# Identity products in TensorE's waits, keys asked for by GpSimd, and one scaling moved, in a fused delta-rule and maxout kernel

## Chip, core and metric

The kernel runs on one core of one Trainium2 chip. The metric is the device time of one execution in microseconds (us), as a median over runs. Engines are called as in the profile: PE (TensorE's matrix multiplications, with PEld for its weight loads), DVE (VectorE), ACT (ScalarE), POOL (GpSimd) and SP (SyncE, which here only issues DMAs).

## What is computed

A delta-rule attention is followed by a feed-forward layer with a maximum over three products. All is float32.

```python
# q, k, v: (4, 8, 768, 48); beta: (4, 8, 768)
k_n = k / (np.linalg.norm(k, axis=-1, keepdims=True) + 1e-06)
state = 0                                  # (4, 8, 48, 48)
for t in range(768):
    y[:, :, t] = q[:, :, t] @ state        # by batch and head
    v_old = state applied to k_n[:, :, t]
    state += beta[t] * outer(k_n[:, :, t], v[:, :, t] - v_old)
x = y.transpose(0, 2, 1, 3).reshape(3072, 384)
h = np.maximum(np.maximum(x @ w1, x @ w2), x @ w3)   # 384 -> 768
out = h @ w_out                                      # 768 -> 384
```

## The kernel before

The sequence of 768 steps is cut into 12 chunks of 64. Within a chunk the recurrence becomes small matrix products and a triangular inverse. A chunk has two units (n = 2c and 2c+1), each of two batches by eight heads; four units (two chunks) make a group, and there are six groups, m = 0 to 5. A group's 512 tokens then go through the feed-forward layer, `ffn(m)`.

The order on every engine is written out by hand, in the order in which the Python code emits instructions. There are three stretches.

The opening, before the first `ffn`, loads keys, turns them (`turn`, p_t), forms products of keys with keys and queries (`gram` and `keys`, p_g), and inverts the first group's triangles in `solve(0)`, a chain of small DVE steps (L570 and L574). ACT and DVE copy the inverse into `ut` (L589, L591); POOL does so for the second chunk. Half blocks are then joined: `halves_z` (p_e), `halves_u` (p_f, with the negations L686 on DVE and L688 on ACT), `join_z` (p_z), `join_u` (p_j). `new` makes the new values u (p_u), `to_y` the outputs (p_y), `to_x` turns these into `xt` (p_x, copied by L880 on ACT and L881 on DVE).

`ffn(0)` is a generator with 31 periods, i = 0 to 30. In each it emits one hidden product, p_h (L930), with its copy or maximum (L938 on ACT, L944 on DVE), or one output product, p_o (L962). Between two of them the loop places links of the recurrence, from two tables: `FIRST` (group 0 and the keys and queries of the first units) and `EARLY_LINKS` (group 1). A letter with a number is one link: `z1` is `join_z(1)`, `k1` is `old_k(1)` (p_k), `T2` turns the queries of unit 2, `P2` forms their products, `S1` makes one step of `solve`. The loop also converts the weights from 64-bit floats piece by piece (`weights`: ACT L232 and L241, POOL L236, DVE L251 and L255, POOL L259; a piece's last three steps come with the following piece), loads keys, and scales a chunk's values by the norms of its keys (`prep_values`, POOL L292 on `v_t`). It makes solve(2), and the subtractions `less_first` (L887).

The later `ffn(m)`, m = 1 to 5, take their links from `LINKS`. There, POOL loads the keys (L118) and values (L137), and both SP and POOL load turned blocks (L401). `p1` in `LINKS` calls `prep_values` for the group ahead; for a chunk that has been scaled before, it does nothing.

`kpad` holds the keys of eight units: unit n lies in place n mod 8 for n below 12. So unit 8 takes the place of unit 0, which `step(0)` (p_s, L795) reads last. PSUM has two buffers for p_h, p_o and the filler products (`ps_ffn`), and three of two banks for the others (`ps_two`).

`busy(n, of)` multiplies the identity with `of` n times into one PSUM tile that nobody reads. The kernel before calls it once, at the very start, with 6.

Of the kernel before, what the change touches and what calls it, by code (L numbers as in the profile page):

```python
# [21 lines left out]
def kernel(  # L22
# [105 lines left out]
    def load_k(n, queues=one_queue):  # L128
        load(k, kpad[place(n)], n, queues)
# [167 lines left out]
    def prep_values(c):  # L297

        if c in nrms:
            scale(c, nrms.pop(c))  # L300
# [37 lines left out]
    def first_norms():  # L338
        norm(nrm_0, ksum_0, small("root0", 2, 2, H), small("newton0", 2, 2, H))
# [7 lines left out]
    def by_par(t):  # L347
        return t.rearrange("p (j two) x -> p two j x", two=2)
# [77 lines left out]
    def masked(t, of, engine=nc.vector):  # L426
        engine.tensor_tensor(  # L427
            out=by_par(t), in0=of,
            in1=mask[:, None, None, :].to_broadcast([128, 2, NP, C]), op=ALU.mult,
        )  # L430

    def gram(n, parts=(0, 1), queues=one_queue, copy=nc.scalar.copy, later=False):
        kqt, g = kqts[n], n % 2
        p_g = ps_two("p_g")

        whole = len(parts) == 2 and not g
        for j in range(NP):
            for par in range(2):
                for bb in range(2):
                    kq = kqt[dims(par), j, bb ^ g]  # L440
                    for i in (0,) if whole else parts:
                        c0 = j * 128 + i * C
                        nc.tensor.matmul(  # L443
                            p_g[
                                rows(bb ^ (g * i)), par, c0 : c0 + C * (1 + whole)
                            ],
                            kq[:, 0],
                            kq if whole else kq[:, i],
                        )
        p_v = p_g.rearrange("p two (j i t) -> p two j i t", j=NP, i=2)  # L450
        if 1 in parts:
            pt = pts[n] = square("pt")
            if later:
                copy(by_par(pt), p_v[:, :, :, 1])
            else:
                masked(pt, p_v[:, :, :, 1])
        if 0 not in parts:
            return
        at = ats[n] = square("at")
        copy(by_par(at), p_v[:, :, :, 0])  # L460
        if queues:
            to_dram(n, queues)
# [171 lines left out]
    def turn_t1(c):  # L634

        t, u_t = t1[c % NU], ut[c % NU]
        nc.vector.transpose(out=t[:, 0], in_=u_t[:, 0, :, 0:BL])
        for bb in range(2):
            nc.vector.transpose(
                out=t[block(1 - bb), 1], in_=u_t[block(bb), 1, :, 0:BL]  # L640
            )
# [28 lines left out]
    def halves_z(c):  # L670
        if c > 1:
            halves_t(c)
        at = [ats[2 * c + g] for g in range(2)]
        second = ut[c % NU].rearrange("p g h (f two x) -> p g h f two x", two=2, x=HB)
        for hs, p_v, copy in heads_of(c, "p_e", BL):
            for i, h in enumerate(hs):
                for bb, g in TILES:
                    r = rows(bb)
                    nc.tensor.matmul(
                        p_v[rows(bb ^ g), g, i], at[g][r, h], second[r, g, h, :, 1]  # L680
                    )
            copy(zs[c % NU][:, :, span(hs)], p_v)
# [7 lines left out]
    def halves_u(c):  # L690
        t, z = fine.pop(c), zs[c % NU]
        for hs, p_v, _ in heads_of(c, "p_f", BL):
            for i, h in enumerate(hs):
                for bb, g in TILES:
                    r = rows(bb ^ g)
                    nc.tensor.matmul(p_v[rows(bb), g, i], t[g][r, h], z[r, g, h])
            for f in (0, 1):
                for bb in range(2):
                    r = block(bb, f, HB)
                    negated(  # L700
                        bb,
                        ut[c % NU][r, :, span(hs), BL * f + HB : BL * (f + 1)],
                        p_v[r, :, :, HB * f : HB * (f + 1)],
                    )

    def join_z(c):
        at = [ats.pop(2 * c + g) for g in range(2)]
        z, second = zs[c % NU], ut[c % NU][:, :, :, BL:C]
        for hs, p_v, _ in heads_of(c, "p_z", BL):
            for i, h in enumerate(hs):  # L710
                for bb, g in TILES:
                    r = block(bb, 1)
                    nc.tensor.matmul(  # L713
                        p_v[block(bb ^ g), g, i], at[g][r, h, 0:BL], second[r, g, h]
                    )
            nc.scalar.copy(z[block(0), :, span(hs)], p_v[block(0)])
            copy = nc.vector.tensor_copy if c < 2 else nc.scalar.copy
            copy(z[block(1), :, span(hs)], p_v[block(1)])

    def join_u(c):  # L720
        z, t = zs[c % NU], t1[c % NU]
        u12 = ut[c % NU][:, :, :, BL:C]
        for hs, p_v, _ in heads_of(c, "p_j", BL):
            for i, h in enumerate(hs):
                for bb, g in TILES:
                    r = block(bb ^ g)
                    nc.tensor.matmul(p_v[block(bb), g, i], t[r, g, h], z[r, g, h])  # L727
            for bb in range(2):
                negated(bb, u12[block(bb), :, span(hs)], p_v[block(bb)], c)
# [36 lines left out]
    def new(c):  # L766
        rhs = rhss.pop(c)
        u = us[c] = both("u", D, 2)
        for hs, p_v, copy in heads_of(c, "p_u", D):
            for i, h in enumerate(hs):  # L770
                for bb, g in TILES:
                    nc.tensor.matmul(  # L772
                        p_v[rows(bb ^ g), g, i],
                        ut[c % NU][rows(bb), g, h],
                        rhs[rows(bb), g, h],
                    )
            copy(u[:, :, span(hs)], p_v)
        if c + NU < 2 * FINE:
            for bb in range(2):
                corner = ut[c % NU][block(bb), :, :, BL:C]  # L780
                zero = kpad[0][block(bb), None, 0:1, D : D + 1]
                nc.scalar.copy(corner, zero.to_broadcast(corner.shape))
# [193 lines left out]
    def some(gen, n):  # L976
        for _ in range(n):
            if next(gen, gen) is gen:
                break
# [59 lines left out]
    keys(7)  # L1039
    turn(1, (1,))  # L1040
    gram(1, (1,), None, later=True)
    for _ in range(2):
        fetch(nc.sync)
    blocks(1)
# [3 lines left out]
    some(solving, HB + 1)  # L1048
    halves_t(0)
    halves_z(0)  # L1050
    first_norms()
    for c in range(2):
        scale(c, nrm_0[:, c])
    some(conv, 1)
    halves_u(0)
    turn_t1(0)
    join_z(0)
    masked(pts[0], by_par(pts[0]))
    join_u(0)
    masked(pts[1], by_par(pts[1]))  # L1060
    old_k(0)
    old_q(0)
    some(solving, 1)
    new(0)
    some(conv, 1)
    fetch(nc.sync)
    to_y(0)
# [1 line left out]
    fetch(nc.sync)  # L1069
    halves_z(1)  # L1070
    to_x(0)
    some(conv, 1)
    fetch(nc.sync)
    halves_t(1)
# [18 lines left out]


    FIRST = {
        0: "f1 s0 T2 S1 S1", 1: "z1 d1 S1 k1 P2 T3 S1 S1", 2: "j1 S1 S1 S1",
        3: "P3 S1 q1 S1 S1", 4: "u1 T4", 5: "y1", 6: "s1 T5 P4", 7: "x1 T6",
        8: "P5 T7", 10: "P6", 12: "P7",
    }
# [5 lines left out]
    )  # L1105
    MADE = dict(V=load_v, P=prep_values)
    UNIT = dict(t=turn, g=gram, K=load_k, L=lambda n: load_blocks(n, nc.sync))
    OF_KEYS = dict(S=lambda n: some(solving, n), T=lambda n: turn(n, (1,)), P=lambda n: gram(n, (1,)))

    def links(m, names):  # L1110
        for name in names.split():
# [23 lines left out]
    for i, _ in enumerate(ffn(0)):  # L1135
        if i - 1 in CONVERTED:
            fetch(nc.sync)
        queries(FIRST.get(i, ""))
        links(1, EARLY_LINKS.get(i, ""))
        if i in CONVERTED:  # L1140
            some(conv, 1)
        if i in (4, 5, 6):
            some(solving, (4, 2, 1)[i - 4])
        if i in (5, 7):
            prep_values(i // 2)
        if 7 <= i < 11:
            load_k(i + 1)
        if i == 0:
            load_v(3)
        if i == 12:  # L1150
            load_q(11)
        if i in (10, 18):
            load_v(4 + i // 18)
        if i == 18:
            blocks(2)
        if i == 21:
            solving = solve(2)
            some(solving, 1)
        if i in (22, 25):
            prep_values(4 + i // 25)  # L1160
        if 21 < i < 27:
            some(solving, 3)
        if i >= 27:
            some(solving, 4 if i < 30 else 5)
        if i in (27, 28, 29):
            load_blocks(i - 15, nc.sync)
        if i in (18, 19, 20, 22, 25, 27):
            less_first((18, 19, 20, 22, 25, 27).index(i))
        if 27 <= i < 30:
            turn_first((2 * (i - 27), 2 * (i - 27) + 1))  # L1170
# [48 lines left out]
```

## Time and profile before

| | us |
|---|---|
| median of 6 runs | 544.28 (542.42 to 547.78) |
| the profiled execution's own time | 544.39 |
| its span | 542.7 |
| PE busy | 505.6 (93%) |
| DVE busy | 317.2 (58%) |
| POOL busy | 178.9 (33%) |
| ACT busy | 154.6 (28%) |
| mean granted PE clock | 0.955 of full speed |

The span is what the records of the profile cover; the profiled execution took 1.7 us more. A row of the order of time reads: start, duration, engine, line and operation, what is written from what, shape and count, and in brackets the idle time before it with what ended it. A row of a table of stretches reads: the stretch, its length, then busy time and number of instructions on PE, PEld, DVE, ACT and POOL, then the granted PE clock, the DMA engines' busy share and GB/s.

### The profile page before, as it was taken

What the parts mean: (1) busy time and instruction counts of PE and PEld (TensorE: products, weight loads), DVE (VectorE), ACT (ScalarE), POOL (GpSimd) and SP (SyncE); (2) the same over time, 40 slices, a digit from 0 to 9 for tenths busy, and PEclk for the clock granted to TensorE, in tenths of its full rate; (3) what the DMA queues carried; (4) which work ended last, traced back from release to release, by engine and by line L of the source; (5) the groups of instructions that cost most, each with busy time, mean ns of one, the idle gap of its engine ahead of it and who ended that gap; (6) DMA issues with size and microseconds to landing.
All of it is one profiled execution on the core that took longest, in us unless ns stands there. A gap on an engine that the chain in (4) does not pass through costs nothing.

```text
span 542.7 us, 18538 instructions
## 1 busy us (share of the span) xinstructions
PE 505.6 (93%) x8096; PEld 312.7 (58%) x8096; DVE 317.2 (58%) x701; ACT 154.6 (28%) x285; POOL 178.9 (33%) x303
## 2 busy tenths in 40 slices
PE   6657788999979999999999999999999999999996
PEld 5546677876536555556654566565565555654453
DVE  5877898776899552199762489661989313101100
ACT  5536364575302233210133220153101331010100
POOL 7216146234293280665093766231330000000000
PEclk9756898999989999999997999999999999999999
DMA  8882847885024591544393546474323402130011
GB/s 110 186 164 77 150 116 166 177 197 132 17 55 103 129 179 28 120 121 116 86 180 67 126 116 148 107 128 87 89 71 77 80 2 57 49 73 1 0 22 36
DMA packets 118848, 53.49 MB, mean 99 GB/s; under 512 B 100976, under 2 KB 113456, under 8 KB 118768
## 3 DMA queue, kind: packets, MB, share of 16 engines
q1 hardware_dynamic: 109872, 40.01, 34.7%
q0 software_dynamic: 6784, 11.92, 9.9%
q8 instruction: 63, 1.03, 0.8%
q10 hardware_dynamic: 2112, 0.39, 0.5%
q14 instruction: 17, 0.14, 0.1%
HBM read 39.17 MB, written 13.11 MB: 96 GB/s over the span
## 4 chain that ended last, share of the span: by engine, by line
PE 78%; DVE 13%; ACT 3%; issue 3%; DMA 2%; SPq 1%; POOL 0%; ACTq 0%; DVEq 0%; POOLq 0%
PE p_h L930 35%; PE p_o L962 25%; PE p_g L443 3%; PE p_m L910 2%; DVE tmp L570 2%; PE p_y L814 2%; PE p_u L772 2%; PE p_k L744 2%; PE p_q L744 2%; SPq L118 1%; PE p_j L727 1%; PE p_s L795 1%; DVE y_bl L574 1%; DMA kmore<-in_k_dram 1%; PE p_z L713 1%
## 5 line engine op out<-in xcount | busy, mean ns | idle before, releaser
L930 PE MATMUL p_h<-xt,w_sb 128*128 128x512 f32 (+1 forms) x522 | 222.3, 571 | 7.9 <-DVE h L944 3.6
L930 PEld LDWEIGHTS p_h<-xt,w_sb 128*128 128x128 f32 x522 | 97.3, 195 | 95.9 <-issue 86.8
L962 PE MATMUL p_o<-wo_sb,h 128*128 128x384 f32 x288 | 97.8, 489 | 0.0
L944 DVE TENSOR_TENSOR h<-h,p_h 128x512 f32<-128x512 f32 (+1 forms) x48 | 29.6, 618 | 95.8 <-PE p_h L930 95.7
L962 PEld LDWEIGHTS p_o<-wo_sb,h 128*128 128x128 f32 x288 | 53.7, 190 | 35.7 <-issue 0.5
L570 DVE TENSOR_TENSOR tmp<-x_bl,y_bl 128x31 f32<-128x31 f32 (+20 forms) x139 | 51.5, 371 | 4.1
L968 ACT COPY o_sb<-p_o 128x384 f32<-128x384 f32 x24 | 11.5, 478 | 140.6 <-PE p_o L962 134.5
L574 DVE TENSOR_TENSOR y_bl<-y_bl,tmp 128x31 f32<-128x31 f32 (+20 forms) x139 | 47.5, 342 | 4.8
L940 ACT ACTIVATE h<-p_h 128x512 f32<-128x512 f32 x30 | 17.9, 597 | 91.0 <-PE p_h L930 86.7
L962 PE MATMUL p_o<-w_sb,xt 128*128 128x384 f32 x120 | 42.0, 486 | 0.0
L401 POOL DMA_DIRECT2D turned<-in_q_dram x72 | 39.1, 550 | 4.7 <-POOL turned L396 2.6
L443 PE MATMUL p_g<-kqt 48*64 48x64 f32 (+1 forms) x1216 | 29.7, 241 | 10.9 <-DVE nt_bl L268 3.7
L443 PEld LDWEIGHTS p_g<-kqt 48*64 48x64 f32 x1216 | 25.1, 141 | 18.6 <-ACT kqt L372 7.8
L962 PEld LDWEIGHTS p_o<-w_sb,xt 128*128 128x128 f32 x120 | 22.8, 190 | 15.9
L427 DVE TENSOR_TENSOR pt<-p_g,mask 128x512 f32<-128x512 f32 x22 | 15.2, 691 | 20.3 <-PE p_g L443 20.1
L292 POOL TENSOR_TENSOR v_t<-v_t,nrm 128x768 f32<-128x768 f32 x12 | 17.8, 1489 | 27.9 <-DVE nrm L271 13.5
L236 POOL TENSOR_SCALAR mant<-mant 128x384 f32<-128x384 f32 x24 | 13.1, 547 | 41.5 <-ACT mant L232 41.5
L802 DVE TENSOR_TENSOR st<-st,p_s 48x768 f32<-48x768 f32 (+1 forms) x18 | 17.1, 950 | 15.4 <-PE p_s L795 15.2
L137 POOL DMA_DIRECT2D v_t<-in_v_dram x12 | 9.9, 830 | 41.8 <-PE p_u L772 41.8
L259 POOL TENSOR_TENSOR w_sb<-mant,up 128x384 int32<-128x384 int32 x18 | 17.9, 997 | 12.8 <-DVE mant L255 12.8
L396 POOL MEMSET turned<- 128x96 f32 x18 | 3.3, 193 | 53.9 <-DVE kqt L417 53.9
L118 POOL DMA_DIRECT2D kpad<-in_k_dram x24 | 16.3, 687 | 11.5 <-PE p_s L795 11.5
(151 smaller groups left out, 621.6 us busy)
## 6 DMA issues: line engine op xcount, KB each, us to landing
w_bits<-in_moe_w_dram SPq DMA_DIRECT2D x18, 384.0 KB, 5.8
out_dram<-o_sb SPq DMA_DIRECT2D x48, 96.0 KB, 2.2
turned<-in_q_dram POOLq DMA_DIRECT2D x72, 48.0 KB, 2.6
y_x<-y SPq DMA_DIRECT2D x16, 192.0 KB
qall<-y_x SPq DMA_DIRECT2D x32, 96.0 KB, 3.0
at_d<-at SPq DMA_DIRECT2D x80, 32.0 KB, 2.2
ut<-y_d SPq DMA_DIRECT2D x40, 64.0 KB, 2.6
qall<-in_q_dram SPq DMA_DIRECT2D x24, 96.0 KB, 3.9
```

What stands on the lines that cost most here:

```text
L118: queues[bb].dma_start(out=dst[rows(bb ^ g), :, 0:D], in_=src[2 * bb + g, :, c * C : (c + 1) * C, :].rearrange("h p d -> p h d"),)
L259: nc.gpsimd.tensor_tensor(out=dst.bitcast(I32), in0=mant_v.bitcast(I32), in1=up_v, op=ALU.add)
L292: nc.gpsimd.tensor_tensor(out=vts[c], in0=vts[c], in1=nrm[:, :, :, None].to_broadcast([128, 2, H, D]), op=ALU.mult,)
L401: (queue, nc.gpsimd)[i].dma_start(out=t[p0 : p0 + 32, bb, at : at + NP * 2 * D].rearrange("p (j x) -> p j x", j=NP), in_=(k, q)[i][2 * bb ...
L443: nc.tensor.matmul(p_g[rows(bb ^ (g * i)), par, c0 : c0 + C * (1 + whole)], kq[:, 0], kq if whole else kq[:, i],)
L570: nc.vector.tensor_tensor(out=t_v, in0=row.to_broadcast(t_v.shape), in1=column.to_broadcast(t_v.shape), op=ALU.mult,)
L574: nc.vector.tensor_tensor(out=rest, in0=rest, in1=t_v, op=ALU.subtract)
L744: nc.tensor.matmul(p_b[rows(bb), par, c0 : c0 + D], kqt[g][dims(par), j, bb ^ g, i], st[dims(par), bb ^ g, g, j],)
L930: nc.tensor.matmul(p_h, w_sb[i][:, t, f * 128 : (f + 1) * 128], xt[:, t, lo : lo + w], start=(t == 0), stop=(t == KT - 1),)
L940: nc.scalar.activation(out=h, in_=p_h, func=mybir.ActivationFunctionType.Relu)
L944: nc.vector.tensor_tensor(out=h, in0=h, in1=p_h, op=ALU.max)
L962: nc.tensor.matmul(p_o, stays, moves, start=(n == 0), stop=(n == len(terms) - 1))
```

## The change

Three things are done in one edit. First, `busy` is called at more places: seven in the opening, with 49 products in all, and, by a new letter `B` in `FIRST`, 4 and 6 in period 1 of `ffn(0)`. Second, the keys of units 8 to 11 are asked for by POOL, those of units 8 and 9 in period 1 and those of 10 and 11 in period 7; before, SP asked for them one unit a period in periods 7 to 10. Third, the values of chunk 5 are no longer scaled in period 25 of `ffn(0)`; `p1` of `LINKS` does it in period 5 of `ffn(1)`.

```diff
@@ opening
     gram(1, (1,), None, later=True)
+    busy(22, ident)
     for _ in range(2):
         fetch(nc.sync)
...
     halves_z(0)
+    busy(4, ident)
     first_norms()
...
     halves_u(0)
+    busy(4, ident)
     turn_t1(0)
     join_z(0)
+    busy(2, ident)
     masked(pts[0], by_par(pts[0]))
     join_u(0)
+    busy(7, ident)
     masked(pts[1], by_par(pts[1]))
...
     new(0)
+    busy(4, ident)
     some(conv, 1)
     fetch(nc.sync)
     to_y(0)
...
     to_x(0)
+    busy(6, ident)
     some(conv, 1)
@@ links of ffn(0)
-        0: "f1 s0 T2 S1 S1", 1: "z1 d1 S1 k1 P2 T3 S1 S1", 2: "j1 S1 S1 S1",
+        0: "f1 s0 T2 S1 S1", 1: "B4 z1 d1 S1 k1 P2 B6 T3 S1 S1", 2: "j1 S1 S1 S1",
...
-    OF_KEYS = dict(S=lambda n: some(solving, n), ...
+    OF_KEYS = dict(B=lambda n: busy(n, ident), S=lambda n: some(solving, n), ...
@@ loop of ffn(0)
-        if 7 <= i < 11:
-            load_k(i + 1)
+        if i in (1, 7):
+            for n in range(2):
+                load_k(8 + 2 * (i > 1) + n, (nc.gpsimd, nc.gpsimd))
...
-        if i in (22, 25):
-            prep_values(4 + i // 25)
+        if i == 22:
+            prep_values(4)
```

More of the change, by code (lines that the diff above doesn't have):

```diff
@@ L1107 @@
     UNIT = dict(t=turn, g=gram, K=load_k, L=lambda n: load_blocks(n, nc.sync))
-    OF_KEYS = dict(S=lambda n: some(solving, n), T=lambda n: turn(n, (1,)), P=lambda n: gram(n, (1,)))
+    OF_KEYS = dict(B=lambda n: busy(n, ident), S=lambda n: some(solving, n), T=lambda n: turn(n, (1,)), P=lambda n: gram(n, (1,)))
     def links(m, names):
```

## The prediction

> **What bounds the kernel now.** I read the page first, then stretches of 2 us over the opening, the waits of TensorE, and the order of time on TensorE, VectorE and GpSimd around each wait.
>
> ```profile
> span 542.7 us, 18538 instructions
> ...
> PE   6657788999979999999999999999999999999996
> ...
> PEclk9756898999989999999997999999999999999999
> ...
> q8 instruction: 63, 1.03, 0.8%
> ```
>
> TensorE (PE) is busy 93% of the span and nearly always from about 88 us on. Only the opening, one dip near 150 us and one near 285 us have room. PE's waits, from the answer on waits (us in all, times, longest):
>
> ```profile
> PE p_e L679 <- ACT ut L589: 4.7, 2, 4.1
> PE p_h L930 <- DVE h L944: 3.6, 2, 2.9
> PE p_h L930 <- issue: 2.0, 1, 2.0
> PE p_j L727 <- issue: 1.8, 1, 1.8
> ```
>
> The stretches show the opening's second trouble: after the hole at 26 us the granted clock (third figure from the right) is a half.
>
> ```profile
> 24.00:26.00 2.00, 1.33 (x52) 1.02 (x44) 1.77 (x7) 1.14 (x2) 0.00 (x0) 1.00 0.29 49
> 26.00:28.00 2.00, 0.23 (x15) 0.05 (x4) 1.81 (x6) 0.58 (x1) 0.00 (x0) 0.51 0.43 60
> 28.00:30.00 2.00, 0.00 (x0) 0.00 (x0) 1.93 (x3) 0.79 (x1) 0.00 (x0) 0.50 0.46 67
> ...
> 48.00:50.00 2.00, 2.00 (x42) 1.89 (x35) 1.46 (x2) 1.29 (x3) 1.32 (x3) 0.52 0.69 195
> 50.00:52.00 2.00, 0.75 (x5) 0.52 (x4) 1.21 (x3) 1.81 (x5) 1.34 (x2) 1.00 0.49 115
> ```
>
> It stays a half until 49.9 us; p_f, p_z, p_u, p_y, p_e and p_x run there at about twice their later times (p_u 2.35 us against 1.15, p_y 1.96 against 1.15). From 52 to 83 us the chain of waits is VectorE (DVE) nearly throughout (1.8 to 2.0 busy in every 2 us), after that PE. At 150 us, in order of time:
>
> ```profile
> 149.59 2.91 POOL L292 TENSOR_TENSOR v_t<-v_t,nrm 128x768 f32<-128x768 f32 x2
> 149.74 1.40 DVE L574 TENSOR_TENSOR y_bl<-y_bl,tmp 128x60 f32<-128x60 f32 x1
> 151.17 1.43 DVE L570 TENSOR_TENSOR tmp<-x_bl,y_bl 128x87 f32<-128x87 f32 x1
> 153.74 0.68 DVE L944 TENSOR_TENSOR h<-h,p_h 128x512 f32<-128x512 f32 x1
> 154.56 7.08 PE L930 MATMUL p_h<-xt,w_sb 128*128 128x512 f32 x12 [2.95 <-DVE h L944]
> ```
>
> Two tiny DVE steps last as long as the two scalings on GpSimd (POOL) beside them; elsewhere the same steps take 0.22 to 0.25 us. L944 comes late for it, and PE stands 2.95 us, then runs at half clock from 155.7 to 159.1.
>
> [...] the trace's changes (15.78, 22.61, 26.02, 49.91, 63.57, 66.98, 84.05, 87.46, ...) lie whole multiples of 3.41 us apart. Windows busy 1.97 to 2.14 us out of 3.41 went either way; the ones that restored the clock were busy throughout. [...] the added products are ordinary matmuls, and no run so far shows 22 of them. [...] PE's "issue" waits at 39.6, 61.7, 107.4, 201.3 and 283.5 us come after 1217, 2241, 4289, 7361 and 9921 recorded instructions, all 193 above a multiple of 256. From the entry into one block to the next being there took 2.6 to 4.9 us where it was waited for (7.1 once, in the opening); a PE that runs 256 small instructions faster than that stands.
>
> **The change part by part.** All is added to the profiled execution, 544.39 us with a span of 542.7; the median of the six runs is 544.28, so 0.1 lower.
>
> *Fillers in the opening (49 identity products: 22, 4, 4, 2, 7, 4, 6).* A product is two passes. At half clock the opening's 12 passes started over 2.72 us: 0.453 us a product. At full clock four transposes of 128 columns start over 0.46 us (121.61 to 122.07): 0.115 a pass, 0.23 a product. The 22 start at 26.2 us, after the last p_g, and p_e can start in earnest at 31.4, when L589 has both pieces. At full clock they end at 26.2 + 5.1 = 31.3. In the profiled phase of the windows the clock falls at 26.02 and comes back at 29.43: 7 products at 0.453, 15 at 0.23, end 32.9. By the windows' phase I take full clock in about 7 of 10 executions. What follows is then set by others: the transposes t (until 33.55), then L267 to L271 and the alternating L686/L688 (until 37.0), then L637/L639 and L718 (38.9); p_f and p_z at double speed plus 4 + 4 + 2 fillers (2.3 us) fit between. p_j starts at 38.9 as before, but without its 1.79 us of "issue" ends by 39.7 to 40.6 instead of 42.1. Seven fillers (1.6 us) hide under L686/L688; p_u ends near 43, p_y near 44.5 (47.2 before). Late next is POOL: v_t of chunk 1 lands at 42.04 by DMA, then L292, L236, L591 keep POOL until 46.1, L236 and L259 until 47.6 (48.7 before). ACT's L232, L241, L682 and L880 queue behind that, so xt comes 1.0 us earlier, and with it the DVE chain to 83 us. The fillers before p_h (6, 1.4 us) lie under L880/L881. Against this: the overrun to 32.9 and a block boundary now inside p_z (128 more instructions stand ahead of p_j), which can put p_j back to 42: +0.6. I take **−0.5** (−1.0 to +4).
>
> *Fillers in period 1 (4 and 6).* The 4 lie in the 1.34 us before p_z, which waits for DVE's L686 either way. The 6 take 1.4 us in place of an "issue" wait of 1.2, before p_t; if they hold the clock at 63.6 us, the next p_h saves 1.1 us, but DVE, not PE, ends the chain there. **0** (−0.3 to +1.5, the latter if the next block is late just there and p_j, then L688 and L686, move).
>
> *Keys 8 to 11 on POOL.* Eight issues leave SP (0.63 us each, between 94 and 105 us) and join POOL (0.68 each by its later L118 rows): four after L259 of period 1 (70.0 to 72.8), four after L292 of period 7 (92.7 to 95.5). Behind the first four stands L236 (70.73, now 72.8); the DVE reads it at 75.9. L259 after it moves from 73.08 to 73.3, and ACT's L232 by 0.25 us. kpad 0 and 1 were last read by p_s at 56.6, kpad 2 and 3 by p_s at 80.6, so no issue waits. Behind the second four stands L236 until 96, read at 99.5. The keys are first turned at 99.98, without a wait before. SP's next transfers go out up to 5 us earlier, but L473 waits for ACT's copies. **0** (−0.3 to +0.5).
>
> *Chunk 5.* One of the two L292 leaves 149.6 to 152.5: L570 at 151.17 falls from 1.43 to 0.25 us, so L944 and p_h come 1.2 us earlier; the wait is 1.77 us. It may or may not cost a half-clock window (12 p_h took 7.08 us against 5.54): I take 3 chances in 10 to save 1.54. **−1.6** (−2.7 to −1.0). In its new place, behind v_t's load near 193 us, POOL has 15.5 us of wait at 203 to 219[...]. No cost.
>
> *The blocks move.* 59 products are 236 instructions, so every later boundary falls 20 instructions later than an old one. Near 94 us a block now covers p_k and p_q alone (2.5 us, where 4 are needed): +1.2. Near 112: +0.3. Near 284 the boundary goes from the first p_h record to 10 records later:
>
> ```profile
> 283.49 0.70 PE L930 MATMUL p_h<-xt,w_sb 128*128 128x512 f32 x1
> 286.15 4.63 PE L930 MATMUL p_h<-xt,w_sb 128*128 128x512 f32 x5 [1.96 <-issue]
> 290.71 1.82 PE L727 MATMUL p_j<-z,t 32*32 32x32 f32 x128
> ```
>
> PE gets there at about 286.3, when the block is in. That saves 2.2 us of wait and, at full clock, 2.3 on the five p_h and 0.5 on p_j; the next block is then short (2.2 us), +1.8, with an even chance of half clock, +0.6. So −2.6 there, **−1.1** in all (−4 to +3).
>
> Sum: −0.5 + 0 + 0 − 1.6 − 1.1 = −3.2 on the profiled 544.39: 541.2; the median's 0.1 stays in the rounding. About 0.5% (2.7 us) is what a measurement here can tell from no change.
>
> **The rivals.** (1) *Slower: fillers at half clock.* If identity products don't restore the clock, 22 of them last 22 × 0.453 = 10 us and end at 36.2 instead of 31.4: p_e, and the chain behind it to the DVE stretch, come 4.8 us later: 544.4 + 4.8 − 1.6 = 547.6. It decides from an end of the 22 past about 35.6. For it: half clock at 26.02 in the trace. Against: windows that were full before did restore it. (2) *No difference: the opening is DVE's and POOL's, and the blocks only change places.* Then chunk 5 alone acts, 1.2 to 1.6: 542.9. For it: DVE 1.9 of 2 us from 52 to 83. Against: the 5 us at 284 are two rows of the trace. That the fillers might be removed as unused is excluded: they stand in the built order.
>
> **How the numbers follow.** Forecast 541.2: 0.50, a quarter of it short of 0.5%. Rival 2: 0.30, a few of them over 0.5%. Rival 1, with late blocks at 36, 62 or 94 us adding up likewise: 0.20, the mild ones inside 0.5%. That gives faster 0.44, same 0.39, slower 0.17. The range 537.5 to 547 leaves out about 1 in 20 below (both clock windows saved and no new block wait) and 1 in 8 above.
>
> **What would show it.** Right: 22 products end between 31 and 33 us at clock 1.0; xt (L880) about 1 us earlier; one L292 near 150 us and p_h's wait there below 2 us; no "issue" wait at p_h near 284. Wrong: p_e after 35 us, DVE idle before L251 near 70 to 76 us, "issue" waits of 2 us or more at p_z or p_q.

## The result, and the profile after

The changed kernel takes 547.89 us (median of 36 runs), the kernel before 544.27 in the same comparison (73 runs). The ratio is 1.0056 with a 95% interval of 1.0037 to 1.0075: slower by 0.6%, about 3.0 us, where 541.2 was forecast and 547.0 was the upper end of the range. Medians hold all runs and ratios only undisturbed ones, so the sizes below are worked out from ratios (on 544.4 us); the profiled executions of e3_fill_256, e4_tiny_236 and e6_keys lie 3.7 to 5.4 us above those kernels' medians, so only the places of waits are read from them.

The page of the changed kernel, its first lines and the queue that brings instructions:

```profile
span 546.1 us, 18785 instructions
...
PE   8688898798989998999999999999999999999996
...
PEclk9899798988999999999999999999999999999999
...
q8 instruction: 64, 1.05, 0.8%
```

The profiled execution took 547.78. The opening did become what the fillers were to make it: PE's first slices went from 6657788 to 8688898, and the mean granted clock from 0.955 to 0.979. The span is 3.4 us longer all the same. PE's own answer on waits (us in all, times, longest) says where to look:

```profile
PE p_g L443 <- issue: 3.8, 2, 2.1
PE p_h L930 <- DVE h L944: 2.4, 2, 1.8
...
PE p_f L696 <- issue: 2.1, 1, 2.1
...
PE p_e L679 <- issue: 1.6, 1, 1.6
...
PE p_h L930 <- issue: 0.6, 1, 0.6
```

"issue" is time in which PE waited for nothing that the profile shows. As in the trace of before, such waits (seven of 0.3 us or more here) come 193 or 194 recorded instructions above a multiple of 256, and the instruction queue moves packets of 16,384 bytes, 64 for 16,428 matmuls and weight loads (before: 63 for 16,192). So I read each of them as the place where one block of 256 instructions ends and the next is not there yet. The wait for L944 is smaller than before (2.4 against 3.6), the "issue" wait of 1.8 us at p_j is gone, and that of 2.0 at p_h is down to 0.6. New are one of 2.1 us at p_f and one of 1.6 at p_e, and p_g waits 3.8 in all for "issue", where before it was 2.3. The order of time on PE shows them in place:

```profile
26.44 5.18 PE L993 MATMUL p_w<-ident 128*128 128x128 f32 x44
...
33.11 1.12 PE L679 MATMUL p_e<-ut,at 64*64 64x32 f32 x60 [0.77 <-ACT ut L589]
...
63.76 0.49 PE L443 MATMUL p_g<-kqt 48*64 48x64 f32 x7 [2.13 <-issue]
64.17 2.93 PE L993 MATMUL p_w<-ident 128*128 128x128 f32 x12
...
103.42 0.90 PE L679 MATMUL p_e<-ut,at 64*64 64x32 f32 x48 [1.57 <-issue]
...
109.78 0.67 PE L696 MATMUL p_f<-z,t 64*64 64x32 f32 x32 [2.07 <-issue]
...
210.12 0.59 PE L443 MATMUL p_g<-kqt 48*64 48x128 f32 x10 [1.63 <-issue]
...
285.95 2.84 PE L930 MATMUL p_h<-xt,w_sb 128*128 128x512 f32 x6
...
296.35 1.02 PE L930 MATMUL p_h<-xt,w_sb 128*128 128x512 f32 x2 [0.56 <-issue]
```

The same places in before, where p_e and p_f run through:

```profile
63.15 0.80 PE L443 MATMUL p_g<-kqt 48*64 48x64 f32 x28 [1.20 <-issue]
...
98.92 1.14 PE L679 MATMUL p_e<-ut,at 64*64 64x32 f32 x64
...
102.82 1.15 PE L696 MATMUL p_f<-z,t 64*64 64x32 f32 x64
...
202.29 0.76 PE L443 MATMUL p_g<-kqt 48*64 48x128 f32 x17 [0.74 <-issue]
```

Now set record against record: the start of each matrix product in this trace, less the start of the same product in the trace of before (times up to 100 us are those of before, later ones those of the change). The changed kernel is 0.4 to 0.6 us ahead at 51 to 61 us, and 3.0 behind at 64 to 67; 2.2 to 2.5 behind at 78 to 98; 4.3 at 102, 6.5 at 108, 8.1 after a half-clock window at 110.4, 9.6 after another at 127.4. Chunk 5 returns 2.9 near 160; the site near 208 takes 0.9 more than it took before; the site of before's 284 returns 4.9, close to the 5.0 that its step had worked out, and 0.7 of that is lost again at the wait behind it; 3.4 are left at the end. A half-clock window is a stretch at a granted clock of 0.5; in both traces the clock changes at times that lie whole multiples of 3.41 us apart (in the change at 18.21, 21.63, 62.59, 69.41, 86.48, 89.89, 110.37, 113.79, 127.44 and 130.85).

At 62 us the boundary of a block of instructions lies 25 products into p_g instead of 4. The wait there grew to 2.13 us from 1.20, and the clock fell before the six fillers came (stretches of 2 us; the granted clock is the third figure from the right):

```profile
60.00:62.00 2.00, 1.55 (x89) 1.47 (x90) 1.86 (x8) 0.69 (x2) 0.28 (x2) 1.00 0.96 173
62.00:64.00 2.00, 0.24 (x7) 0.24 (x6) 1.91 (x5) 0.00 (x0) 0.95 (x1) 0.65 0.26 55
64.00:66.00 2.00, 2.00 (x15) 1.88 (x12) 1.92 (x5) 0.00 (x0) 0.00 (x0) 0.50 0.49 164
```

So the six fillers took 2.93 us behind the wait, and VectorE, which sets the pace there (1.91 and 1.92 us busy in the last two of these stretches), stood for the p_h behind them:

```profile
70.07 0.42 DVE L944 TENSOR_TENSOR h<-h,p_h 128x256 f32<-128x256 f32 x1 [1.72 <-PE p_h L930]
71.38 0.69 DVE L686 TENSOR_SCALAR ut<-p_j 32x512 f32<-32x512 f32 x1 [0.89 <-ACT ut L688]
```

The scaling of chunk 5, in order of time on POOL, DVE and PE, is one L292 shorter, and only one small step of DVE is stretched beside it now:

```profile
159.21 1.47 POOL L292 TENSOR_TENSOR v_t<-v_t,nrm 128x768 f32<-128x768 f32 x1
159.36 1.40 DVE L574 TENSOR_TENSOR y_bl<-y_bl,tmp 128x60 f32<-128x60 f32 x1
160.79 0.25 DVE L570 TENSOR_TENSOR tmp<-x_bl,y_bl 128x87 f32<-128x87 f32 x1
162.18 0.68 DVE L944 TENSOR_TENSOR h<-h,p_h 128x512 f32<-128x512 f32 x1
163.00 5.39 PE L930 MATMUL p_h<-xt,w_sb 128*128 128x512 f32 x12 [1.77 <-DVE h L944]
```

### The profile page after: what moved, and what is told of

It is laid out like the page before. It is cut to its first block, busy times and chain, and to the rows that moved or that the text cites. A ratio compares the mean times of both kernels' runs of the same rounds, so it can differ in the third digit from the quotient of the medians.

```text
span 546.1 us, 18785 instructions
## 1 busy us (share of the span) xinstructions
PE 514.6 (94%) x8214; PEld 323.9 (59%) x8214; DVE 316.8 (58%) x701; ACT 154.8 (28%) x285; POOL 184.6 (34%) x311
## 3 DMA queue, kind: packets, MB, share of 16 engines
q8 instruction: 64, 1.05, 0.8%
## 4 chain that ended last, share of the span: by engine, by line
PE 80%; DVE 9%; issue 3%; ACT 3%; DMA 2%; SPq 1%; POOL 1%; DVEq 0%; ACTq 0%; POOLq 0%
PE p_h L930 34%; PE p_o L962 24%; PE p_g L443 5%; PE p_m L910 2%; PE p_k L744 2%; PE p_t L366 2%; PE p_u L772 2%; PE p_y L814 2%; PE p_q L744 2%; DMA v_t<-in_v_dram 1%; PE p_j L727 1%; PE p_s L795 1%; DVE tmp L570 1%; PE p_z L713 1%; DMA kpad<-in_k_dram 1%
## 5 line engine op out<-in xcount | busy, mean ns | idle before, releaser
L930 PE MATMUL p_h<-xt,w_sb 128*128 128x512 f32 (+1 forms) x522 | 220.0, 566 | 4.4 <-DVE h L944 2.4
L944 DVE TENSOR_TENSOR h<-h,p_h 128x512 f32<-128x512 f32 (+1 forms) x48 | 29.7, 618 | 97.0 <-PE p_h L930 96.9
L574 DVE TENSOR_TENSOR y_bl<-y_bl,tmp 128x31 f32<-128x31 f32 (+20 forms) x139 | 49.5, 356 | 4.8
L570 DVE TENSOR_TENSOR tmp<-x_bl,y_bl 128x31 f32<-128x31 f32 (+20 forms) x139 | 48.7, 350 | 4.1
L292 POOL TENSOR_TENSOR v_t<-v_t,nrm 128x768 f32<-128x768 f32 x12 | 17.9, 1493 | 24.9 <-DVE nrm L271 13.6
L118 POOL DMA_DIRECT2D kpad<-in_k_dram x32 | 21.9, 692 | 12.3 <-PE p_s L795 12.3
L993 PE MATMUL p_w<-ident 128*128 128x128 f32 x130 | 19.6, 309 | 2.0 <-POOL ident masks.py:199 2.0
```

The costliest lines, as they stand in the source:

```text
L118: queues[bb].dma_start(out=dst[rows(bb ^ g), :, 0:D], in_=src[2 * bb + g, :, c * C : (c + 1) * C, :].rearrange("h p d -> p h d"),)
L292: nc.gpsimd.tensor_tensor(out=vts[c], in0=vts[c], in1=nrm[:, :, :, None].to_broadcast([128, 2, H, D]), op=ALU.mult,)
L570: nc.vector.tensor_tensor(out=t_v, in0=row.to_broadcast(t_v.shape), in1=column.to_broadcast(t_v.shape), op=ALU.mult,)
L574: nc.vector.tensor_tensor(out=rest, in0=rest, in1=t_v, op=ALU.subtract)
L930: nc.tensor.matmul(p_h, w_sb[i][:, t, f * 128 : (f + 1) * 128], xt[:, t, lo : lo + w], start=(t == 0), stop=(t == KT - 1),)
L944: nc.vector.tensor_tensor(out=h, in0=h, in1=p_h, op=ALU.max)
```

## The experiments

**One part alone, and all but one.** e5_chunk5 has the last hunk of the change alone, e6_keys the hunk of the keys alone, e2_fill_only all calls of `busy` alone. e1_no_fill is the change without them, e7_fill_chunk5 the change with the keys left on SP.

```diff
 e6_keys
-        if 7 <= i < 11:
-            load_k(i + 1)
+        if i in (1, 7):
+            for n in range(2):
+                load_k(8 + 2 * (i > 1) + n, (nc.gpsimd, nc.gpsimd))
 e5_chunk5
-        if i in (22, 25):
-            prep_values(4 + i // 25)
+        if i == 22:
+            prep_values(4)
```

> The change without any filler product: keys 8 to 11 on POOL and chunk 5 later. Theory 1 (the 236 added instructions move TensorE's block boundaries into short stretches): boundaries lie as before, so the waits at 62, 201 and 283 us are there as before, none of 1.5 us or more at p_e and p_f near 101 to 108; time 1 to 3 us below before, from chunk 5. Theory 2 (the fillers cost by the TensorE time they take) gives the same time. Theory 3 (the keys on POOL crowd the DMA engines near 100 us, so that blocks of instructions come late): a block that comes 3 us or more after entry near 100 us, DMA share above 1.1 there, and no gain or a loss against before.

> The fillers alone; keys stay on SP, chunk 5 where it was. Theory 1: the wait of about 2 us in p_g near 62 us and the waits near 94 to 108 us as in the changed kernel, no wait at p_h near 284; time as the changed kernel plus about 1.2 to 2.7 for chunk 5, so 3 to 6 us above before. Theory 3: the wait at 62 us stays, those at 101 and 107 us (1.57 and 2.07) shrink below 1, DMA share there under 1.1; time within 1 us of before.

> Chunk 5 alone. All theories: the wait of p_h for L944 near 154 us falls from 2.95 to about 1.8; time 1.2 to 2.7 us below before (the larger figure where the half-clock window behind the wait goes too).

> The keys of units 8 to 11 on POOL alone. Theory 3 (SP, free of them, asks for weights and queries earlier, just while POOL asks for the last keys; the DMA engines are crowded near 100 us and a block of instructions comes late): DMA share of 1.1 or more between 98 and 108 us, a block there that lands 3 us or more after entry, TensorE waits of 1 to 3 us, time 1 to 4 us above before. Against it: time within 0.5 us of before.

> The change with the keys left on SP: 59 full fillers and chunk 5. Theory 3: the late blocks near 100 us go, so below the changed kernel by 1 to 3 us. The shift of 236 (theory 1) stays: 1 to 3 us above before, the fillers' 3.5 less the 2.7 of chunk 5.

| kernel | median us | before, same chip | ratio (95% interval) | in us |
|---|---|---|---|---|
| e2_fill_only | 548.57 | 544.45 | 1.0058 (1.0031 to 1.0085) | +3.2 |
| e6_keys | 547.04 | 544.48 | 1.0045 (1.0018 to 1.0073) | +2.4 |
| e5_chunk5 | 541.73 | 544.48 | 0.9960 (0.9932 to 0.9988) | -2.2 |
| e1_no_fill (keys, chunk 5) | 543.58 | 544.45 | 1.0003 (0.9971 to 1.0034) | +0.2 |
| e7_fill_chunk5 (fillers, chunk 5) | 544.52 | 543.41 | 1.0013 (0.9989 to 1.0036) | +0.7 |
| the change | 547.89 | 544.27 | 1.0056 (1.0037 to 1.0075) | +3.0 |

The parts add up as far as the intervals tell, which reach 1.0 to 1.7 us to either side: 3.2 + 2.4 - 2.2 = 3.4 against 3.0; keys and chunk 5 give 0.2 as their sum does (0.2), fillers and chunk 5 give 0.7 (sum 1.0). So the loss has two sources of similar size, and the third part brings what it was to bring. e7_fill_chunk5 was expected 1 to 3 us above before and came out a little below that. It shows the two sources apart on PE. With the keys on SP the p_e near 102 us runs through, while the wait at p_g near 64 stays:

```profile
66.25 0.34 PE L443 MATMUL p_g<-kqt 48*64 48x64 f32 x7 [2.43 <-issue]
...
102.23 1.26 PE L679 MATMUL p_e<-ut,at 64*64 64x32 f32 x64
```

In e5_chunk5 the DVE step is short, as in the change, and no half clock follows it:

```profile
153.48 0.25 DVE L570 TENSOR_TENSOR tmp<-x_bl,y_bl 128x87 f32<-128x87 f32 x1
155.69 5.39 PE L930 MATMUL p_h<-xt,w_sb 128*128 128x512 f32 x12 [1.76 <-DVE h L944]
```

The other traces agree. In all seven kernels with the scaling moved this p_h waits 1.76 or 1.77 us, with full clock behind it. In the seven with the scaling in place it waits 2.94 or 2.95, and in six of them a half-clock window follows.

**The number of instructions, without the work.** `tiny(n)` issues products of 32 by 32 by 32, each with a 64th of a filler's multiplications, so that the block boundaries move and PE gets next to no work; the mean granted clock stays near before's 0.957 to 0.958 (medians of the runs: 0.954 in e4 and 0.958 in e9, against 0.978 in e2). e4_tiny_236 puts 59 of them where the change puts its 59 fillers (236 instructions: 16,428 matmuls and weight loads in the change, 16,192 in before); e9_tiny184 puts 46 at one place of the opening (184 instructions). I chose 184 from the trace of before: sliding blocks of 256 over its recorded order, it was the shift at which the blocks' run times fell least short of 4 us, my estimate from the 2.6 to 4.9 us that late blocks had taken (2.7 us in all, by steps of four instructions); 236 falls 6.9 us short, 41st of the 64 shifts. e3_fill_256 is the change with five tiny products behind its last six fillers: 256 instructions, one whole block. e8_tiny184_chunk5 adds the chunk-5 hunk to e9.

```diff
+    def tiny(n):
+        p_w = ps_ffn([128, TOK], "p_w")[0:32, 0:32]
+        for _ in range(n):
+            nc.tensor.matmul(p_w, ident[0:32, 0:32], ident[0:32, 0:32])
...
     gram(1, (1,), None, later=True)
+    tiny(46)
```

> The changed kernel with 5 more products of 32x32x32 behind the 6 fillers, so that 256 instructions are added and every later boundary lies where it lay before. Theory 1: from period 1 on the waits of before return (201 and 283 us, with the half clock after 283), those at p_e and p_f near 101 to 108 us go; time 1 to 3 us below the changed kernel. Theory 2: no change against the changed kernel. Theory 3: blocks still come late near 100 us; time within 1 us of the changed kernel.

> The kernel before with 59 products of 32x32x32 at the places of the fillers: the same 236 instructions, hardly any TensorE time and no warm clock. Theory 1: waits of 1 us or more at p_g near 62 us and no wait at p_h near 284, as in the changed kernel; time 1 to 5 us above before. Theory 2: within 1 us of before. Theory 3: within 1 us of before.

> Chunk 5, and 46 products of 32x32x32 at 26 us, that is 184 instructions instead of 236. Theory 1 (only the places of the block boundaries count): from the block lengths in the trace of before, 184 is the shift with the least waiting, about 4 us less than before and 7 less than with 236; so 3 to 7 us below before. If boundaries do not matter: as chunk 5 alone.

> The 46 tiny products alone, nothing else. Theory 1: 2 to 5 us below before, no waits of 1 us or more in p_g near 62 and 201 us or at p_h near 284. If boundaries do not matter, or extra instructions cost as such: within 1 us of before or above it, like the 59 tiny products.

| kernel | median us | before, same chip | ratio (95% interval) | in us |
|---|---|---|---|---|
| e4_tiny_236 | 547.98 | 544.45 | 1.0028 (0.9994 to 1.0061) | +1.5 |
| e9_tiny184 | 540.95 | 544.48 | 0.9949 (0.9924 to 0.9974) | -2.8 |
| e8_tiny184_chunk5 | 539.55 | 544.48 | 0.9935 (0.9906 to 0.9964) | -3.5 |
| e3_fill_256 | 547.89 | 544.45 | 1.0046 (1.0014 to 1.0078) | +2.5 |

e9_tiny184 is the plain case: products that nobody uses make the kernel 0.5% faster. In its trace no block comes late at 284 us any more (order of time on PE in e9):

```profile
277.90 2.84 PE L930 MATMUL p_h<-xt,w_sb 128*128 128x512 f32 x6
...
282.98 2.41 PE L930 MATMUL p_h<-xt,w_sb 128*128 128x512 f32 x5
```

Record against record, e9 is 0.3 us ahead of before at 202 us and 5.4 at 292. Near 62 us its p_g is not cut either, though a wait of 0.78 stands at the p_h behind. With 236 instructions p_g waits 5 to 6 us in all for "issue" (2.3 in before), near 61, 113 to 115 and 206 to 209 us (answer on waits of e4_tiny_236, then of e2_fill_only):

```profile
PE p_g L443 <- issue: 5.9, 3, 2.3
```

```profile
PE p_g L443 <- issue: 5.3, 4, 2.2
```

So e4's tiny products reproduce the fillers' waits at 61, 113 to 115 and 206 to 209. Their time does not settle how much of the fillers' +3.2 is the shift: +1.5 has an interval from -0.3 to +3.3, while by the medians of all runs e4 lies 3.5 above before and e2 4.1. What e4 lacks besides is the fillers' own work, 2.93 us behind the wait near 64. e3_fill_256 was to bring before's boundaries back for everything after period 1. It did: it waits 0.47 us near 208 and 1.93 near 291, as before does at nearly the same places of the program (0.74 and 1.96). It was no faster than the change: what it won at 208 it lost again at 291, which is before's 284, its largest wait, and the keys' wait near 106 stayed (3.3 us at p_f).

**What the keys collide with.** e11_keys_spread keeps them on POOL but asks for one unit a period, in SP's old periods 7 to 10. e12_keys_sp_held asks for them as the change does and gives SP eight loads of 64 bytes in their old places, so that it stays occupied.

```diff
 e11_keys_spread
         if 7 <= i < 11:
-            load_k(i + 1)
+            load_k(i + 1, (nc.gpsimd, nc.gpsimd))
 e12_keys_sp_held, beside the hunk of e6
+        if 7 <= i < 11:
+            for bb in range(2):
+                bit = const.tile([1, 16], FP32, name=f"bit{i}_{bb}")
+                nc.sync.dma_start(out=bit, in_=k[0, 0, 0:1, 0:16])
```

> The keys of units 8 to 11 on POOL, but one unit a period in periods 7 to 10, as SP had them; nothing else. If it is asking for four units in two bunches that crowds the DMA engines, blocks near 100 us come in time and the time is within 0.5 us of before. If it is SP running ahead once it has no keys to issue, the crowding and 1 to 3 us above before stay.

> The kernel before with the keys of units 8 to 11 asked for by POOL as in the change, and at SP's old places in periods 7 to 10 eight loads of 64 bytes each, so that SP stays as occupied with issues as before (nothing reads what they bring). Theory (SP, freed of eight issues, runs ahead and crowds the DMA engines near 98 to 108 us, and instruction blocks land late): DMA share at 98 to 108 us falls from 1.21 to about 0.85, the waits for instructions near 95 to 106 us fall from 4.3 us in all to 1.5 or less, and the time is 544 to 545. Rival (it is POOL's issues, or the keys' earlier place, that cost): the time stays near 547 and the waits stay. A third case, small loads delay the queue by themselves: waits on SP's later transfers and a time above 547.

e11_keys_spread: 550.39 us against 543.41, ratio 1.0127 (1.0083 to 1.0171), in six runs, three at 547.5 to 548.0 and three at 552.8 to 553.5; that is more than either of its expected cases. e12_keys_sp_held: 544.75 against 543.64, ratio 1.0027 (1.0004 to 1.0051). The stretch from 98 to 108 us (length, granted clock, the DMA engines' busy share, GB/s; the share sums the times of all packets over 16 engines and passes 1 where packets overlap, 1.18 in the change) reads so in before, in the change, in e6, e11, e7 and e12, one fence each:

```profile
98.00:108.00 10.00, 1.00 0.82 180
```

```profile
98.00:108.00 10.00, 1.00 1.18 194
```

```profile
98.00:108.00 10.00, 1.00 1.21 175
```

```profile
98.00:108.00 10.00, 0.98 1.21 187
```

```profile
98.00:108.00 10.00, 1.00 0.81 186
```

```profile
98.00:108.00 10.00, 1.00 0.91 184
```

Beside the share I summed what PE waited at block boundaries between 90 and 110 us, counting steps over 0.5 us from one matmul's start to the next:

| | DMA share, 98 to 108 | waits at boundaries, 90 to 110 us |
|---|---|---|
| keys on POOL: e1, e3, e6, e11, the change | 1.14, 1.16, 1.21, 1.21, 1.18 | 4.3, 4.2, 4.3, 4.6, 4.6 |
| keys on SP: before, e2, e4, e5, e7, e8, e9, e10 | 0.82, 0.93, 1.02, 1.02, 0.81, 0.78, 1.00, 0.93 | 0.6, 0.7, 0.8, 1.7, 0, 1.8, 1.2, 2.2 |
| e12, SP held | 0.91 | 3.1 |

The two groups don't touch, whatever the fillers are. Two things qualify this. The rate does not tell the groups apart (175 to 194 GB/s with the keys on POOL, 167 to 193 on SP): no more data moves in the stretch, but its packets take longer in sum. And the table counts boundaries alone. In e2, e4, e5 and e10 PE also waits 1.1 to 2.4 us there for the keys themselves (p_t at L366 for `kpad`), which no kernel with the keys on POOL does. With all its waits PE stands 0.1 to 3.4 us between 90 and 110 us with the keys on SP, and 3.6 to 4.3 with them on POOL.

The packets of PE's instruction queue show where the late blocks lose their time. In the keys' group the transfer of a late block starts 3.0 to 5.4 us after the block before it is entered: in the change the block before is entered at 96.66 and the transfer starts at 100.07, then 103.42 and 106.98; in e11, 99.34 and 104.76, and PE stands 3.9 us. Before has 2.1 for the one it waited for (103.19, 105.31), and no kernel with the keys on SP has more than 3.4 at these blocks. The transfer itself takes 1.1 to 1.7 us there, and 0.9 to 1.7 with the keys on SP. So it is a late start more than a slow transfer that sets the late blocks apart. The order of time on SP tells how the share rises: although its PE is 4 us or more behind there, the change sends v_t out at 103.77 against 104.87 and the next piece of the weights at 107.04 against 107.37; before spends 102.16 to 104.83 on keys. In e6, on PE:

```profile
101.60 1.02 PE L679 MATMUL p_e<-ut,at 64*64 64x32 f32 x57 [1.27 <-issue]
...
107.68 0.98 PE L696 MATMUL p_f<-z,t 64*64 64x32 f32 x40 [1.79 <-issue]
```

With SP held, in e12:

```profile
100.17 1.14 PE L679 MATMUL p_e<-ut,at 64*64 64x32 f32 x64
...
105.64 0.55 PE L696 MATMUL p_f<-z,t 64*64 64x32 f32 x24 [1.07 <-issue]
```

The share fell as expected (0.91), p_e runs through, and the wait at p_f is 1.07 instead of 1.79. Of the waits, expected at 1.5 us or less from 95 us on, 1.3 stand there. The other part of e12's 3.1 us, 1.8 at 93.5, lies before POOL issues units 10 and 11 (93.78); e5, whose keys are on SP, has 1.7 there too. The time, 0.3% above before, lies between e6's 0.45% and nothing; its interval takes in the first and stops just short of the second. e11 says that it is not the bundling of POOL's issues: spread out, they cost more. So that SP's head start crowds the engines is supported, not proved, and why e11 lost more than e6 is open. A rival that no run separates is the form of the transfers: by the pages' queue lines the keys take 384 packets on POOL's queue and 4224 on SP's, for nearly the same bytes.

**A version that beats both.** e10_fill184_chunk5 keeps 46 real fillers, all in the opening (19, 4, 4, 2, 7, 4, 6; 184 instructions), keeps the chunk-5 hunk and leaves the keys on SP.

```diff
-    busy(22, ident)
+    busy(19, ident)
...
-        0: "f1 s0 T2 S1 S1", 1: "B4 z1 d1 S1 k1 P2 B6 T3 S1 S1", 2: "j1 S1 S1 S1",
+        0: "f1 s0 T2 S1 S1", 1: "z1 d1 S1 k1 P2 T3 S1 S1", 2: "j1 S1 S1 S1",
```

> 46 full filler products (19, 4, 4, 2, 7, 4, 6 in the opening, none in period 1) and chunk 5, keys on SP: 184 instructions, so from period 0 of the first feed-forward layer on the boundaries of the 46 tiny ones. If the warm clock in the opening is worth anything at the end, it is faster than the 46 tiny products with chunk 5 (539.6) by 0.5 us or more; if filling as such is neutral, within 1 us of it; if the fillers cost by their time, above it. By theory 1 in any case 3 to 6 us below before.

539.31 us against 543.41, ratio 0.9911 (0.9881 to 0.9942). Beside e8_tiny184_chunk5 (0.9935, 0.9906 to 0.9964) the intervals overlap: that real products are better than tiny ones is not shown. In its profiled execution a late block at 37.2 us (1.8 us) was followed by half clock from 37.8 to 44.7 in spite of the fillers.

## Why the prediction was wrong, point by point

**Fillers in the opening: the clock came as worked out, the time did not.** The 22 products ran at full clock (1.00 from 26 to 32 us) and ended at 31.62 (26.44 + 5.18; 31.3 in the working). p_e at 33.11 waited for L589, not for them. p_j lost its "issue" wait of 1.79. xt's copy L880 came at 49.86 instead of 50.24: 0.4 earlier, not 1.0, close to the -0.5 of the sum. But that was one execution and a lucky one. e2, e3 and e7 have the same opening; there L880 comes at 49.69, 52.00 and 52.07, and in the six kernels without added products at 49.84 to 50.74. In e3 and e7 the wait at the block boundary inside p_z put p_j back to 41.77 and 41.34, near the 42 of the working, and the seven fillers behind p_j ran at half clock, which the working did not count (e7; two rows are one product: 0.48 us each, against 0.235 for the 22 in the change):

```profile
39.62 0.64 PE L713 MATMUL p_z<-ut,at 32*32 32x32 f32 x30 [1.72 <-issue]
...
42.35 3.36 PE L993 MATMUL p_w<-ident 128*128 128x128 f32 x14
```

So in two of these four executions the opening gained a little, and in two it lost more than 1 us: no gain is shown. The 7 in 10 for full clock was my estimate from the places of the 3.41-us windows; they lie differently in the profiled executions of before and the change (edges at 22.61 us in before, 21.63 in the change). A higher mean clock was not a shorter time.

**Fillers in period 1: this step failed.** It had the six take 1.4 us "in place of an 'issue' wait of 1.2". The wait did not go: 49 + 4 products are 212 instructions, which puts the boundary 44 instructions, 22 products, later in the same p_g. That could have been counted from the change. The wait grew to 2.13, the fillers came after it at half clock, and L944 and L686 on DVE passed 2.2 us of it on. "0 (-0.3 to +1.5)" was 2.8 us in this execution, and 1.7 to 2.6 in e2, e3 and e7 (record against record, from 60 to 78 us). The wait is there whenever the 212 instructions are (1.55 to 2.43 us in five kernels; 0 to 1.74 in the six without added products). The fillers' own work behind it counts too: e4, with tiny products in the same places, loses only 0.5 us there.

**The blocks move: right at 284, wrong in sum.** The step for 284 held in each part (no wait, six p_h in 2.84 us; 4.9 us returned, 0.56 of wait behind). Near 94 less came than the 1.2 of the list (0.57 in the change, 0.8 in e4), but near 208 the wait grew from 0.74 to 1.63, a site that the list didn't have, and near 115, where it had 0.3, e2 waits 1.24 and e4 2.07 (the change not at all). Both fillers and blocks, forecast at -1.6 together (-0.5 + 0 - 1.1), measured +3.2 in e2.

**Keys on POOL: the second failed step.** POOL and DVE did hide the issues, as the working said: the four at 70.53 to 73.31 and at 94.90 to 97.67 delayed nothing there. The sentence on SP saw that its next transfers go out earlier and let L473 settle it. It asked who waits for the data and not what else the DMA engines bring: blocks of instructions (64 packets, 1.05 MB). Those came late at 102 and 108 us, and 0 (at most +0.5) measured +2.4. That SP's earlier transfers are what held them up is supported by e12 and not proved.

**Chunk 5: right.** L570 fell from 1.43 to 0.25, the wait from 2.95 to 1.77, as worked out; the half-clock window behind it went as well, which I had given 3 chances in 10 and which went in all seven kernels with this part. -1.6 (-2.7 to -1.0) measured -2.2 in e5. In its new place (199.77 us) no DVE instruction runs beside the scaling.

**The rivals.** That the 22 fillers don't restore the clock (rival 1) did not happen: in e7, where they began at half clock, it came back while they ran, and they ended at 32.95, as the working had it for that case (32.9). Its rider, late blocks adding up, did happen: at 62, as named, and at 102, 107 and 208 us instead of 94, and in e2, e3, e7 and e10 near its 36 us too (37 to 39). It had a fifth of the chance, part of it inside 0.5%. The 541.2 stood on a single favourable site, while every shift draws again at some sixty boundaries. And a range for a shift of 236 instructions should have come from trying neighbouring shifts on before's record.

## What to carry to other kernels

Where TensorE runs long rows of small products, look in the profile for "issue" waits at a fixed count of instructions; here it was 256 (waits 193 or 194 above a multiple). Adding 236 instructions moved every later boundary, 256 put them back (e3), and the shift can outweigh what the added instructions are for (184 instructions without a use gained 0.5%, e9). SP, relieved of the keys, ran ahead (v_t sent out at 103.77 us against 104.87); before calling a moved DMA free, ask what its successors may crowd, the instruction stream included. A higher granted clock is no shorter time by itself: here the mean rose from 0.955 to 0.979 and the kernel became slower.

## What the runs showed of the hardware that was not expected

Instruction blocks are not just late by PE's own pace. With the DMA share of 98 to 108 us at 1.14 or more they cost 4.2 to 4.6 us there in all five kernels, with 1.02 or less 0 to 2.2 in eight, and 3.1 with SP held. The late ones start late: 3.0 to 5.4 us after the block before is entered, and once in, PE takes 1.2 to 2.0 us more to go on. A half-clock window followed the wait of 2.07 us at 109.78 in the change (from 110.4) and those near 108 in e1 and e6, though not the one of 1.57 at 103.42, so a late block can be paid for twice; the second window there, at 127.4 and 125 us, stands behind a wait of 1.4 us for ACT's L372. In before and the change together, from 49.9 to 538 us, PE stood 1.1 us or more in twelve 3.41-us windows at full clock: half clock followed eight of them (1.1 to 2.3 us idle), full clock four (1.3 to 1.6). What starts a fetch stays open: at the site near 208 us it starts at about the entry into the block before in before (199.59 against 199.71) and 0.7 us after it in the change (207.20 against 206.51), takes 1.08 and 1.48 us, and PE waits 0.74 and 1.63.
